# A retention layer and a squared-ReLU feed-forward on one core: another order for the first loads, unread products in TensorE's waits, and two steps moved on ScalarE

## The chip, the core and the metric

The kernel runs on one core of one Trainium2 chip. The metric is the device time of one execution in microseconds (us). Each kernel was executed several times; medians are given with the lowest and the highest. The engines are TensorE (PE in the profile; its weight loads are PEld), VectorE (DVE), ScalarE (ACT), GpSimd (POOL) and SyncE (SP), which issues most loads.

## The reference

```python
# q, k, v: (8, 8, 576, 64) float32;  w_in: (512, 2048) and w_out: (2048, 512) float64
scores = q @ k.T / sqrt(64)                         # for each batch and head
gamma  = 1 - 2.0 ** (-5 - arange(8))                # one per head
ret    = (scores * where(i >= j, gamma ** (i - j), 0)) @ v
x      = ret.transpose(0, 2, 1, 3).reshape(4608, 512)
out    = maximum(x @ w_in, 0) ** 2 @ w_out
```

The decay `gamma ** (i - j)` is split into a factor `gamma ** i` on q and `gamma ** -j` on v. So q has to be multiplied by a table of tokens and heads, and so has v.

## The kernel before

The tokens go through in chunks of 128. For a chunk, TensorE transposes k and q (`turn`), makes the scores (`scores`), and adds up the result from products inside the chunk and a running sum `u` (`retain_a`, `retain_b`, `retain_c`). The first four chunks give the first block of 512 tokens, and only then does the feed-forward have work ("h products", `first_in`). From there on, retention steps and feed-forward steps alternate (`ffn`), with VectorE and ScalarE converting float64 weights between them. A last stage, all of it on the second weight matrix, starts near 602 us.

```python
def load(i):                                   # chunk i, all on SyncE's queue
    for name, src, pool in (("k", k, ld4), ("q", q, ld3), ("v", v, ld4)):
        ...                                    # k and q in three pieces each, v in one
        if i < NCH and name == "q":            # NCH = 5: the q factors, 256 KB a chunk
            nc.sync.dma_start(dq[:, :, c0:c0 + cs], decay_q[:, :, c0:c0 + cs])
    if i == 0:
        nc.sync.dma_start(dv, decay_v)         # the v factors: small

def turn(i):                                   # transposes, then two copies
    ...
    nc.scalar.copy(kT, ...)                                        # ScalarE
    nc.vector.tensor_tensor(qT, ..., dq[...], op=ALU.mult)         # VectorE, scales q

def retain_b(i):
    ...
    # the tiny copy behind which the next products stand ("L458")
    nc.scalar.copy(u_sb[...][:, 0:2, 0:1], xp[0][:, :, cs - CH:cs - CH + 1])

def w_out_parts():                             # conversion of w_out, step by step
    ...
        yield lambda two=two, beside=beside: (two(), beside())     # beside: two ScalarE steps

def ffn(i, half):                              # between the parts of a chunk
    if steps and steps[0][0] == 0:
        step()                                 # four products and ScalarE's relu
        convert(6)                             # conversion of w_in, ScalarE's steps too
        ...

# main loop, first chunks
turn(0)
for i in range(N_CH + 1):
    if i <= N_EARLY:                           # N_EARLY = 4
        ...
        retain_a(i - 1); retain_b(i - 1); retain_c(i - 1)
        scores(i)
        turn(i + 1)
    ...

# last stage: left operands a, four buffers
if n_last in (0, 5, 10):
    fetch_g(n_last // 5)
...
fetch_w2(NP - 1)                               # the last 1.8 MB of weights
fetch_g(3)                                     # the fourth left operand, behind it
```

## Time and profile before

| | before |
|---|---|
| time, first three runs | 1009.67 us (1004.35 to 1010.14) |
| span of the profiled execution | 1004.70 us |
| TensorE busy | 975.3 us, 97% |
| first scores start | 8.29 us |
| first h product starts | 36.41 us |
| ninth h product starts | 42.37 us |
| second stage (later blocks) starts | 114.62 us |
| last product of the second stage ends | 602.25 us |

The last five rows are read from TensorE's timeline, four starts and one end (601.22 + 1.03; the last stage's first product overlaps it, at 602.08). They cut the execution into stages. TensorE is nearly always busy, so a wait of another engine counts only where TensorE stops for it.

These are TensorE's waits in the first 40 us before the change (columns: what waited, what it waited for, us in total, times, longest):

```profile
PE t_ps L373 <- DMA k_ld<-in_k_dram: 4.4, 4, 3.2
PE sc_ps L399 <- DVE qT L381: 2.0, 1, 2.0
PE x_ps L455 <- ACT u_sb L429: 2.0, 4, 0.5
PE x_ps L420 <- ACT u_sb L458: 1.1, 4, 0.3
```

The last two rows are the holes of every chunk, 0.5 and 0.3 us, into which the change puts its unread products.

### The profile page before, as it was taken

The page shows a single profiled execution, that of the slowest core. Times are in us where ns is not written, and L with a number is a line of the kernel's source. Part 1 is how long each engine was busy: PE and PEld are TensorE (multiplying, and loading weights), DVE is VectorE, ACT ScalarE, POOL GpSimd, SP SyncE. Part 2 cuts the span into 40 slices and gives each one's busy share as a digit, 9 for nine tenths or more (in the row PEclk, how much of TensorE's full clock was granted, in tenths as well). Part 3 has the DMA queues.
Part 4 walks back from the last instruction along what each step waited for, and adds up shares of the span by engine and source line. Part 5 has one row for each costly group of instructions (what it writes and reads, how often), then busy time and mean ns, then how long its engine had stood idle before and what let it go on. Part 6 is the DMA issues. An engine that isn't in the chain of part 4 may idle for free.

```text
span 1004.7 us, 24101 instructions
## 1 busy us (share of the span) xinstructions
PE 975.3 (97%) x10376; PEld 862.4 (86%) x10376; DVE 749.7 (75%) x1418; ACT 188.9 (19%) x459; POOL 81.8 (8%) x82
## 2 busy tenths in 40 slices
PE   6999999999999999999999998999999999999998
PEld 4544688888888888788888888999999999999997
DVE  1678797667878888798885776877677677777765
ACT  2344331122222222312311000000000000000000
POOL 1200011011111111111021000000000000000000
PEclk9999999999999999999999999999999999999999
DMA  8974665664786877579566989674764757556351
GB/s 201 241 212 143 183 180 177 171 195 151 207 291 203 239 259 228 139 258 282 150 243 249 401 351 350 252 273 168 252 237 162 273 189 272 187 212 217 119 210 43
DMA packets 187658, 220.34 MB, mean 219 GB/s; under 512 B 119200, under 2 KB 137632, under 8 KB 178592
## 3 DMA queue, kind: packets, MB, share of 16 engines
q1 hardware_dynamic: 187552, 218.81, 66.8%
q8 instruction: 81, 1.33, 0.5%
q14 instruction: 25, 0.20, 0.1%
HBM read 129.39 MB, written 89.39 MB: 218 GB/s over the span
## 4 chain that ended last, share of the span: by engine, by line
PE 87%; DVE 7%; DMA 2%; ACT 2%; SPq 2%; issue 1%; DVEq 0%
PE o_b L800 16%; PE h_b L576 15%; PE o_c L800 11%; PE o_a L800 11%; PE h_a L576 10%; PE h_c L576 9%; PE h_ps L541 6%; PE x_ps L420 3%; PE t_ps L373 2%; PE x_ps L455 2%; DMA a<-g_dram 1%; PE sc_ps L399 1%; DVE room L583 1%; SPq L142 1%; DMA k_ld<-in_k_dram 1%
## 5 line engine op out<-in xcount | busy, mean ns | idle before, releaser
L576 PE MATMUL h_b<-room,w 128*128 128x256 f32 x736 | 177.3, 384 | 1.8 <-DVE room L504 1.2
L576 PEld LDWEIGHTS h_b<-room,w 128*128 128x128 f32 x736 | 137.1, 190 | 22.4 <-DVE room L595 1.4
L800 PE MATMUL o_b<-w,room 128*128 128x128 f32 x1168 | 144.5, 275 | 0.2 <-DVE room L751 0.2
L800 PEld LDWEIGHTS o_b<-w,room 128*128 128x128 f32 x1168 | 137.2, 192 | 0.5 <-DVE room L751 0.4
L800 PE MATMUL o_c<-w,room 128*128 128x128 f32 x1008 | 123.0, 275 | 0.0
L800 PEld LDWEIGHTS o_c<-w,room 128*128 128x128 f32 x1008 | 117.7, 192 | 0.0
L576 PE MATMUL h_c<-room,w 128*128 128x256 f32 x480 | 114.3, 381 | 0.0
L576 PE MATMUL h_a<-room,w 128*128 128x256 f32 x448 | 107.5, 383 | 0.0
L576 PEld LDWEIGHTS h_c<-room,w 128*128 128x128 f32 x480 | 90.5, 190 | 12.5
L576 PEld LDWEIGHTS h_a<-room,w 128*128 128x128 f32 x448 | 83.8, 190 | 11.8
L800 PE MATMUL o_a<-w,a 128*128 128x128 f32 x688 | 85.9, 275 | 2.7 <-DMA a<-g_dram 2.7
L800 PEld LDWEIGHTS o_a<-w,a 128*128 128x128 f32 x688 | 81.3, 192 | 2.9 <-issue 2.9
L593 POOL TENSOR_TENSOR room<-room 128x512 f32<-128x512 f32 x32 | 36.4, 1139 | 435.9 <-ACT room L592 380.7
L583 DVE SCALAR_TENSOR_TENSOR room<-room 128x512 f32<-128x512 f32 x96 | 67.4, 702 | 3.3
L811 ACT COPY r<-o_a 128x128 f32<-128x128 f32 x54 | 14.4, 266 | 276.9 <-PE o_a L800 246.3
L420 PEld LDWEIGHTS x_ps<-ret,v_ld 64*64 64x64 f32 x1152 | 42.5, 143 | 22.8 <-issue 14.1
L420 PE MATMUL x_ps<-ret,v_ld 64*64 64x64 f32 x1152 | 52.4, 234 | 9.1 <-ACT u_sb L458 9.1
L541 PE MATMUL h_ps<-room,w 128*128 128x512 f32 x128 | 59.9, 616 | 0.8 <-ACT room L477 0.7
L595 DVE TENSOR_TENSOR room<-h_b,room 128x512 f32<-128x512 f32 x32 | 22.0, 689 | 42.0 <-PE h_b L576 42.0
L408 POOL TENSOR_TENSOR v_ld<-v_ld,dv 128x512 f32<-128x512 f32 (+1 forms) x40 | 45.0, 1129 | 80.4 <-DMA v_ld<-in_v_dram 67.4
L541 PEld LDWEIGHTS h_ps<-room,w 128*128 128x128 f32 x128 | 24.0, 195 | 27.8 <-issue 25.2
L807 DVE TENSOR_TENSOR small<-o_b,small 128x128 f32<-128x128 f32 x63 | 18.3, 291 | 38.5 <-PE o_b L800 38.4
(94 smaller groups left out, 1369.4 us busy)
## 6 DMA issues: line engine op xcount, KB each, us to landing
g_dram<-room SPq DMA_DIRECT2D x32, 1792.0 KB, 8.1
a<-g_dram SPq DMA_DIRECT2D x43, 1024.0 KB, 7.1
room<-g_dram SPq DMA_DIRECT2D x20, 1024.0 KB, 6.0
w<-w_dram SPq DMA_DIRECT2D x7, 1792.0 KB, 12.1
out_dram<-room SPq DMA_DIRECT2D x18, 512.0 KB, 3.3
v_ld<-in_v_dram SPq DMA_DIRECT2D x32, 256.0 KB, 4.0
w<-in_moe_w_in_dram SPq DMA_DIRECT2D x16, 512.0 KB, 4.9
w<-in_moe_w_out_dram SPq DMA_DIRECT2D x16, 512.0 KB, 4.0
```

Source lines behind the costliest of these rows:

```text
L373: nc.tensor.transpose(p[:, h, j, hp, :], loaded[i][j][rows(h), 2 * hp:2 * hp + 2, :], ident[rows(h), rows(h)])
L408: nc.gpsimd.tensor_tensor(vs[:cs], vs[:cs], dv[:cs, :, ci:ci + 1].to_broadcast([cs, H, D]), op=ALU.mult)
L420: own.append(lambda hp=hp, e=e, b=b: nc.tensor.matmul(x_at(hp, b, h), lhsT=s["vs"][rows(h), 2 * hp + b, :], rhs=s["ret"][rows(h), e, hp, : ...
L455: nc.tensor.matmul(x_at(hp, b, h), lhsT=u[rows(e), hp, :], rhs=s["qT"][rows(e), hp, CH * h:CH * h + CH], start=clears(b, hp // 2), stop=Fa ...
L541: nc.tensor.matmul(p.rearrange("p h t -> p (h t)"), lhsT=w[:, c, :], rhs=xT[0][:, c, :], start=(c == 0), stop=(c == N_DM - 1))
L576: nc.tensor.matmul(p[:, mm, :], lhsT=w[:, c, :], rhs=xs[n][right][:, c, :], start=(j in OPENS and mm == 0 and c == 0), stop=(j in CLOSES a ...
L583: nc.vector.scalar_tensor_tensor(t, t, 0.0, t, op0=ALU.max, op1=ALU.mult)
L593: nc.gpsimd.tensor_tensor(g["A11"], g["A11"], g["A11"], op=ALU.mult)
L595: nc.vector.tensor_tensor(g["A22"], p, p15, op=ALU.add)
L800: nc.tensor.matmul(p, lhsT=s["lefts"][left][:, m, :], rhs=w_out[j][:, m, WO_SLOT[right], :], start=(i in OPENS and m == 0), stop=(i in CLO ...
L807: nc.vector.tensor_tensor(s["u2"], p, s["p1"], op=ALU.add)
L811: nc.scalar.copy(r[:, 0, 0:128], p)
```

## The change

Its intent has five parts. (1) In the first four chunks q is scaled before its transpose by a small table, so that the large table of q factors can be loaded later. Two smaller moves go with it: q is loaded ahead of k, and among the first three chunks one weight piece of 512 KB is fetched instead of two, behind all three. (2) The first k and v are issued by ScalarE's queue beside SyncE's. (3) TensorE makes products that nobody reads ("unread products") in its waits among the first chunks, so that its clock is released from half rate, which the prediction reads from eight equal h products (5.42 us at 36.41 us, 3.70 us at 42.37). (4) Conversion steps of ScalarE are moved so that they don't stand ahead of the tiny copy. (5) The fourth left operand of the last stage is fetched earlier.

```diff
 def load(i):
+    if i == 0:
+        nc.sync.dma_start(dv, decay_v)              # now holds the small q table too
+    if N_EARLY <= i < N_EARLY + NCH:                # the large table, four chunks later
+        nc.sync.dma_start(dq[:, :, c0:c0 + cs], decay_q[:, :, c0:c0 + cs])
-    for name, src, pool in (("k", k, ld4), ("q", q, ld3), ("v", v, ld4)):
+    for name, src in (("q", q), ("k", k), ("v", v)):
     ...
+        issue = nc.scalar if i == 0 and name != "q" else nc.sync
     ...
-        if i < NCH and name == "q":
-            nc.sync.dma_start(dq[:, :, c0:c0 + cs], decay_q[:, :, c0:c0 + cs])

     # start
     for i in range(3):
         load(i)
-        fetch_raw(1 if i else 0)
+    fetch_raw(1)

+def scale_q(i, engine):
+    engine.tensor_tensor(t, t, dv[:, :, NCH + ci:NCH + ci + 1].to_broadcast([C, H, D]), op=ALU.mult)

 # turn
+            elif i < N_EARLY:
+                nc.vector.tensor_copy(to, p[:, :n_h, j, :, :])

 # w_out_parts
-            yield lambda two=two, beside=beside: (two(), beside())
+            yield two, beside                        # held back at the end of a first half
 # ffn
-            step()
-            convert(6)
+            for f in (step, lambda: convert(6)) if half else (lambda: convert(6), step):
+                f()

+def warm(count, wide):                               # unread products
+    t = ps_f.tile([128, 512], F32, tag="f", name="idle_ps")
+    for _ in range(count):
+        if wide:
+            nc.tensor.matmul(t[:, 0:128], lhsT=idle, rhs=idle, start=True, stop=True)
+        else:
+            for b in range(2):
+                nc.tensor.matmul(t[rows(b), 0:64], lhsT=idle[rows(0), rows(b)], rhs=idle[rows(0), 0:64], ...)
 # main loop
+    warm(6, True)
+    scale_q(0, nc.vector)
     turn(0)
     ...
                 retain_a(i - 1)
+                warm(4, False)
                 retain_b(i - 1)
+                warm(4, False)
                 retain_c(i - 1)
     ...
+                if i + 1 < N_EARLY:
+                    scale_q(i + 1, nc.gpsimd)
+                warm(6, False)
                 turn(i + 1)
 # last stage
-            if n_last in (0, 5, 10):
+            if n_last in (0, 5, 10, 15):
                 fetch_g(n_last // 5)
     ...
-    fetch_g(3)
```

Lines of the kernel move by 10 to 38 with the change: the tiny copy L458 is L470 after it, the first copy of qT L381 is L391, the retention products L420 are L432, the h products L541 are L553, the last stage's L800 is L838.

More of the change, by code (lines that the diff above doesn't have):

```diff
@@ L128 @@
     loaded = {}
+    N_EARLY = TOK // C
     def load(i):
         b, ci, c0, cs = chunks[i]
-        got = {}
-        for name, src, pool in (("k", k, ld4), ("q", q, ld3), ("v", v, ld4)):
-            t = got[name] = pool.tile([128, H, D], F32, tag=name, name=f"{name}_ld")
+        got = {name: pool.tile([128, H, D], F32, tag=name, name=f"{name}_ld") for name, pool in (("q", ld3), ("k", ld4), ("v", ld4))}
+        if i == 0:
[3 more added lines that the diff above has]
+        for name, src in (("q", q), ("k", k), ("v", v)):
+            t = got[name]
+            issue = nc.scalar if i == 0 and name != "q" else nc.sync
             at = src[b, :, c0:c0 + cs, :].rearrange("h s d -> s h d")
             if name == "v":
-                nc.sync.dma_start(t[:cs], at)
+                issue.dma_start(t[:cs], at)
             else:
-                nc.sync.dma_start(t[:cs, 0:H // 2, :], at[:, 0:H // 2, :])
+                issue.dma_start(t[:cs, 0:H // 2, :], at[:, 0:H // 2, :])
                 for e in range(2):
-                    nc.sync.dma_start(t[:cs, H // 2 + e::2, :], at[:, H // 2 + 1 - e::2, :])
-            if i < NCH and name == "q":
-                nc.sync.dma_start(dq[:, :, c0:c0 + cs], decay_q[:, :, c0:c0 + cs])
-        if i == 0:
-            nc.sync.dma_start(dv, decay_v)
+                    issue.dma_start(t[:cs, H // 2 + e::2, :], at[:, H // 2 + 1 - e::2, :])
         loaded[i] = [got["q"], got["k"], got["v"]]
@@ L314 @@
     dq = only.tile([128, HP, S], F32, name="dq")
-    dv = only.tile([128, H, NCH], F32, name="dv")
+    dv = only.tile([128, H, 2 * NCH], F32, name="dv")
     exp_bias = const.tile([128, 1], F32, name="exp_bias")
     nc.gpsimd.memset(exp_bias, -896.0 * 2.0 ** 23)
+    idle = only.tile([128, 128], F32, name="idle")
+    nc.vector.memset(idle, 1.0)
     for i in range(3):
         load(i)
-        fetch_raw(1 if i else 0)
+    fetch_raw(1)
     ident = only.tile([128, 128], F32, name="ident")
@@ L333 @@
     u_sb = [only.tile([128, HP, D], F32, name=f"u_sb{j}") for j in range(3)]
-    N_EARLY = TOK // C
     st = {i: {} for i in range(N_CH)}
@@ L363, in clears @@
         return new
+    def scale_q(i, engine):
+        ci, t = chunks[i][1], loaded[i][0]
+        engine.tensor_tensor(t, t, dv[:, :, NCH + ci:NCH + ci + 1].to_broadcast([C, H, D]), op=ALU.mult)
     def turn(i):
@@ L615, in ffn_in @@
         if n >= 3 or n_w2[0] < 3 + 2 * 5:
-            n_w2[0] += 1
-            f = next(w_out_steps, None)
-            f and f()
+            if not (held[0] and type(w_out_next[0]) is tuple):
+                n_w2[0] += 1
+                f = w_out_next[0]
+                w_out_next[0] = next(w_out_steps, None)
+                for f in f if type(f) is tuple else (f,):
+                    f and f()
             if n == N_BLK - 2 and (mp, j) in ((2, 3), (3, 3)):
-                assert f is None
+                assert w_out_next[0] is None
                 fetch_w2(mp - 2)
@@ L626 @@
     w_out_steps = w_out_parts()
+    w_out_next = [next(w_out_steps)]
+    held = [False]
     n_w2 = [0]
@@ L668, in ffn @@
                 break
-        if steps:
+        count = max(1, int(want) - done[0])
+        while steps and count:
+            held[0] = half == 0 and count == 1
             step()
-        while steps and done[0] < int(want):
-            step()
+            count -= 1
+        held[0] = False
+    def warm(count, wide):
[5 more added lines that the diff above has]
+                for b in range(2):
+                    nc.tensor.matmul(t[rows(b), 0:64], lhsT=idle[rows(0), rows(b)], rhs=idle[rows(0), 0:64], start=True, stop=True,
+                                     skip_group_check=True)
+    warm(6, True)
+    scale_q(0, nc.vector)
     turn(0)
@@ L886, in _decays @@
     gv = (gamma[:, None, None] ** -s.astype(np.float64)).transpose(2, 0, 1)
+    order = [h if h < H // 2 else h ^ 1 for h in range(H)]
+    by_s = (gamma[order, None, None] ** s / math.sqrt(D)).transpose(2, 0, 1)
+    gv = np.concatenate([gv, by_s], axis=2)
     return np.ascontiguousarray(gq, dtype=np.float32), np.ascontiguousarray(gv, dtype=np.float32)
```

## The prediction

> **What bounds the kernel now.** I read the page's busy shares first, then its slices, then the table by stretches of time, then what TensorE waited for, and last the timeline around each wait.
>
> ```profile
> span 1004.7 us, 24101 instructions
> ...
> PE 975.3 (97%) x10376; PEld 862.4 (86%) x10376; DVE 749.7 (75%) x1418; ACT 188.9 (19%) x459; POOL 81.8 (8%) x82
> ```
>
> TensorE is busy 975.3 of 1004.7 us, so filling every gap of it is worth 29.4 us at most, and its last product ends some 5 us before the end. A change of the waits is therefore a change of one or two per cent. The table by stretches tells where the gaps are (columns: length, busy time and count for PE, PEld, DVE, ACT, POOL, then granted clock, DMA share, GB/s):
>
> ```profile
> 10.00:15.00 5.00, 3.82 (x85) 3.01 (x88) 0.98 (x2) 1.12 (x3) 1.16 (x2) 1.00 1.02 254
> 20.00:25.00 5.00, 4.27 (x108) 3.67 (x108) 1.49 (x5) 2.33 (x6) 1.34 (x1) 1.00 0.96 234
> 30.00:40.00 10.00, 8.54 (x133) 5.70 (x126) 5.12 (x9) 4.63 (x11) 1.66 (x2) 1.00 0.85 219
> 40.00:50.00 10.00, 10.00 (x53) 4.51 (x51) 7.38 (x13) 3.07 (x5) 2.31 (x2) 1.00 1.02 281
> 200.00:300.00 100.00, 99.98 (x1210) 85.41 (x1210) 74.74 (x125) 22.91 (x51) 14.56 (x14) 1.00 0.66 212
> ```
>
> The first 40 us lose 11.4 us (the stretches of it summed), 40 to 100 lose 3.8, 300 to 500 lose 5.3, around 600 to 620 lose 3, the end 5. Between 120 and 300 nothing is lost. So four places matter. In the first one, the DMA engines are full as well (share 0.92 to 1.02 from 5 to 30 us): the loads are bound there, and TensorE has a second handicap that no share shows:
>
> ```profile
> 7.54 0.69 DVE L381 TENSOR_TENSOR qT<-t_ps,dq 128x512 f32<-128x512 f32 x1 [7.54 <-DMA dq<-in_decay_q_dram]
> ```
> ```profile
> 23.84 0.95 PE L373 MATMUL t_ps<-ident,k_ld 64*128 64x64 f32 x8 [0.27 <-DMA k_ld<-in_k_dram]
> ...
> 36.41 5.42 PE L541 MATMUL h_ps<-room,w 128*128 128x512 f32 x8 [0.68 <-ACT room L477]
> ...
> 42.37 3.70 PE L541 MATMUL h_ps<-room,w 128*128 128x512 f32 x8
> ...
> 46.00 0.46 PE L373 MATMUL t_ps<-ident,k_ld 64*128 64x64 f32 x8
> ```
>
> Eight equal transposes take 0.95 us at 23.84 and 0.46 at 46.00; eight equal products take 5.42 us and then 3.70. Until about 40 us TensorE runs at half its rate, although the granted clock reads 1.00. The first scaled q waits until 7.54 us for the large decay table (dq), which lands after q itself.
>
> The chain puts the start on the issue queue and then on one transfer, the k of the fourth chunk:
>
> ```profile
> 17.64 6.07 DMA k_ld<-in_k_dram
> ```
>
> The other three places, in the waits of TensorE and in the timelines of ScalarE and of the issue queue:
>
> ```profile
> 51.53 0.65 ACT L214 ACTIVATE w<-w 128x512 f32<-128x512 uint32 x1
> 52.07 0.15 ACT L458 COPY u_sb<-x_ps 128x2 f32<-128x2 f32 x1
> ```
> ```profile
> PE x_ps L420 <- ACT u_sb L458: 3.7, 4, 1.1
> ```
> ```profile
> PE o_a L800 <- DMA a<-g_dram: 2.7, 1, 2.7
> ```
>
> The tiny copy L458 releases the next retention products, and it stands in ScalarE's queue behind the weight conversion (L213 0.71 and L214 0.65 us). This costs 3.7 us in 40 to 120, and 3.8 us in 300 to 500 by the same row there. The 2.7 us are the fourth left operand of the last stage: its load is issued at 607.40, behind a 1.8 MB weight load, and lands 14.12 us later by the chain.
>
> [...] the excess 5.42 - 3.70 = 1.72 us is four products at the slow rate (4 x 0.43), or 3.4 us of work. [...] Before, q's first issue is at 2.34 us, after 1.5 us of k's issues, so that is what there is to save.
>
> **The change, part by part.**
>
> *First chunks.* The dq pieces (four of 256 KB and one of 128 KB) leave the front of the queue; the small table goes first, on one queue with q, and k and v of chunk 0 are issued by ScalarE. q is scaled before its transpose, by VectorE for chunk 0 (0.69 us, as L381), by GpSimd for three more (1.06 us each, as L408), off the path if the data is there; L381 becomes a plain copy for four chunks. Chunk 0: q's issue ends near 2.9 us instead of 3.87; it landed 1.9 us after that before, so 4.8; scaling to 5.6; q transposes 1.0 to 6.6; copy 0.7: first scores at about 7.4 instead of 8.29 us. Gain 0.9.
>
> *Unread products.* Before the chunks 12 passes of 128 columns, which lie in the wait of 3.19 us for k. Per chunk 8 + 8 + 12 small products of two passes. They use two column halves side by side, so 28 pairs. A pass of 512 columns takes 3.70 / 8 = 0.46 us fast, so 64 columns take 0.058: 1.6 us a chunk fast, 3.2 us slow (estimates). The real work of a chunk, slow: scores 1.08, transposes 1.78, two inner rounds of 1.1, the outer one 1.14: 6.2 us, which with the waits is the 7.0 us from one chunk to the next (20.17 to 27.18 us). Fast, from 42 to 61 us: 0.69 + 0.76 + 2 x 0.68 + 0.69 = 3.5 us. So a chunk is about 5.2 us if the products release the rate, and about 9.4 if not. I expect release: scores, filler, inner, filler, outer, filler, inner follow each other without a hole for some 7 slow us between transposes[...]. With the first chunk still mostly slow (7.5): scores at 7.4, 14.9, 20.1, 25.3, and the first h product about 5.3 us after the last, at 30.6 instead of 36.41: 5.8 us. The 1.7 us of slow h products go too: 7.5.
>
> Does the DMA let it? Up to the second weight piece 12 loads of 256 KB, two of 512 KB and the table: 4.2 MB, at the 207 GB/s measured over the first 40 us 20 us, plus 2 for the start: 22. The third piece comes 1.0 MB later, at 27, just when VectorE wants it. The dq pieces that were taken out come back before chunks 4 to 8, at 20 to 50 us, where the share is 0.85 to 1.02. So I take off 1.5 us: **6 us** from the front.
>
> *Conversion in 40 to 120.* In the first half-step of each chunk the conversion now goes ahead of the product step, so L213 and L214 run before L458. Comparing ScalarE's order in both programs: before, 10 of 40 copies L458 come directly behind a conversion, four of them in this stage; after, three of 40, none here. Of 3.7 us I take **3**.
>
> *Conversion in 300 to 500.* A step that would end the first half with a conversion is held for the next. Three of the waits (0.33, 1.42, 1.32) lose their cause, one (0.82) stays, and one copy near 462 us newly gets a conversion before it (up to 1 us): **2 us**.
>
> *Last stage.* The fourth left operand is fetched in the last block's 16th of 28 steps, near 580 us, and the DMA has idle time from 596 to 608. So the 2.7 us go: **2.6**.
>
> Sum 6 + 3 + 2 + 2.6 = 13.6 us. The three runs before average 1008.1 us: 994.5.
>
> **Rivals.**
> 1. *TensorE stays slow.* [...] against it is that nothing else stands in the 7 us. Each chunk would then cost 2.4 us more instead of 1.8 less: the front loses 8 or so, and the sum is near zero: 1008 us.
> 2. *The DMA is the bound of the front.* Shares of 0.92 to 1.02 speak for it. Then moved bytes are only paid later: VectorE waits for weight pieces between 30 and 50 us, and the front gives 1 or 2 us: 999 us. Against it: the DMA was half idle for some 3 us near 30 us.
> 3. *The next transfer replaces the last stage's.* The fifth operand's sums already waited 0.79 us at 626.55 for its load, issued at 613.60 into room that a write must leave first. If it is not sooner, only 1.3 us remain: 996 us.
> 4. *All of it without a late weight piece*: 7.5 to 9 in front, 3.7, 3 and 2.7: 989 us.
>
> **Range and chances.** The parts other than the front total 5 to 9 us; the front goes from -8 to +9. The runs before spread over 5.8 us. That makes 987 to 1004 for 8 in 10. Faster by over 2% means under 989.5, which needs the fourth rival: 0.15. Slower by over 2% would need a stall that nothing here points to: 0.02.
>
> **What would show it.** Right: eight transposes of chunk 2 in about 0.5 us instead of 0.95, and the first eight h products in 3.7 us, starting near 31; no wait for dq at the first copy of qT; no wait over 0.4 us of L420 for L458 between 40 and 120; no wait of L800 for the fourth operand. Wrong: first h products still at 5.4 us, or later than 36; VectorE's first conversion step (L205) waiting for its weight load between 25 and 50 us; a new wait near 622 us for the fifth operand.

## The result, and the profile after

| | before | after |
|---|---|---|
| time, four runs each, same rounds | 1008.9 us (1004.35 to 1010.14) | 994.84 us (992.27 to 998.75) |
| span of the profiled execution | 1004.70 us | 990.54 us |

The ratio is 0.9872, with an interval from 0.9825 to 0.9919. A ratio is always the mean time of one kernel's fast runs over that of the other's of the same rounds, so it isn't quite the ratio of the medians. The gain is a little over 1%, and so within the 2% that count as the same.

The changed kernel had nine fast executions, with a mean of 995.2 us and a spread from 992.3 to 998.8. The profiled one is the fastest of the nine, which matters below. One more execution took 1241.73 us at a mean granted clock of 0.754; it was slow from beginning to end, it stayed single, and it isn't used.

The page of the changed kernel, its first lines and its row of instruction loads:

```profile
span 990.5 us, 24582 instructions
...
PE 974.3 (98%) x10612; PEld 866.2 (87%) x10612; DVE 747.5 (75%) x1420; ACT 189.6 (19%) x459; POOL 83.1 (8%) x85
...
q8 instruction: 83, 1.36, 0.6%
```

TensorE has 236 more products (224 records of the small unread ones, two to each, and 12 of the wide ones) and as many more weight loads than before, and yet 1 us less of busy time. What got shorter is the idle time: the span less PE's busy time was 29.4 us and is 16.2 us.

The stages tell where (us; the first two marks are starts, the last two are ends of the last product):

| mark | before | after | stage before | stage after | difference |
|---|---|---|---|---|---|
| ninth h product | 42.37 | 39.07 | 42.37 | 39.07 | -3.3 |
| second stage | 114.62 | 107.25 | 72.25 | 68.18 | -4.1 |
| end of the second stage's products | 602.25 | 591.00 | 487.63 | 483.75 | -3.9 |
| end of the last stage's products | 999.77 | 985.58 | 397.52 | 394.58 | -2.9 |

The table by stretches of time after the change, for the stretches shown of before (length, busy time and count for PE, PEld, DVE, ACT, POOL, then granted clock, DMA share, GB/s), with one stretch more:

```profile
10.00:15.00 5.00, 5.00 (x128) 4.76 (x128) 1.20 (x3) 1.12 (x3) 2.12 (x2) 0.53 1.08 248
20.00:25.00 5.00, 3.48 (x150) 3.21 (x151) 0.95 (x3) 2.75 (x6) 1.06 (x1) 1.00 0.58 146
25.00:30.00 5.00, 5.00 (x154) 4.83 (x148) 4.58 (x8) 2.23 (x6) 1.38 (x1) 0.66 1.01 258
30.00:40.00 10.00, 8.36 (x156) 5.20 (x155) 3.89 (x8) 3.70 (x9) 1.06 (x1) 1.00 0.86 201
40.00:50.00 10.00, 9.92 (x98) 5.07 (x97) 9.79 (x17) 4.78 (x9) 1.06 (x1) 1.00 1.09 321
```

Two things stand out. The unread products fill 10 to 15 us without a hole, but at a clock of 0.53. And 20 to 25 us lose 1.5 us although the DMA engines are only 58% busy there: this hole isn't a transfer. The waits of TensorE in the first 40 us name it:

```profile
PE t_ps L383 <- issue: 1.5, 1, 1.5
PE sc_ps L411 <- DVE qT L391: 1.4, 1, 1.4
PE t_ps L383 <- DMA k_ld<-in_k_dram: 1.2, 1, 1.2
PE x_ps L467 <- issue: 1.1, 2, 0.9
```

"Issue" is a stop in which TensorE waited for nothing that the profile shows. Before the change there was none of any size here. The waits for k, 4.4 us in sum, are down to 1.2, for the most part because unread products now stand in the first of them (without them x2 waits 5.1 us for k); the holes of each chunk are gone; and the stops are new. TensorE's timeline around the first of them (start, length, operation, tiles, count, and in brackets the idle time before it and what ended it):

```profile
20.85 0.87 PE L702 MATMUL idle_ps<-idle 64*64 64x64 f32 x24
21.65 0.40 PE L383 MATMUL t_ps<-ident,k_ld 64*128 64x64 f32 x5
23.57 0.34 PE L383 MATMUL t_ps<-ident,k_ld 64*128 64x64 f32 x3 [1.52 <-issue]
...
34.83 3.70 PE L553 MATMUL h_ps<-room,w 128*128 128x512 f32 x8 [0.68 <-ACT room L489]
...
39.07 3.70 PE L553 MATMUL h_ps<-room,w 128*128 128x512 f32 x8
```

The k of that chunk had landed at 19.18 us, so the eight transposes stop in their middle, with their data there. The first eight h products take 3.70 us instead of 5.42, as predicted, but they start at 34.83 us and not near 31.

The start of VectorE and ScalarE after the change:

```profile
5.88 0.69 DVE L373 TENSOR_TENSOR q_ld<-q_ld,dv 128x512 f32<-128x512 f32 x1 [4.82 <-DMA q_ld<-in_q_dram]
...
7.13 0.58 ACT L389 COPY kT<-t_ps 128x512 f32<-128x512 f32 x1 [2.97 <-PE t_ps L383]
...
7.75 0.69 DVE L391 COPY qT<-t_ps 128x512 f32<-128x512 f32 x1 [1.18 <-ACT kT L389]
```

The wait for the large table is gone, and the first scores still start at 8.50 us instead of 8.29. q is there at 5.76 us, is scaled and transposed, and then the two copies follow one another: VectorE's starts when ScalarE's is about over, which is what its bracket names.

ScalarE near 50 us, where the conversion stood ahead of the tiny copy before:

```profile
47.23 0.60 ACT L557 ACTIVATE room<-h_ps 128x512 f32<-128x512 f32 x1 [1.53 <-PE h_ps L553]
47.73 0.16 ACT L470 COPY u_sb<-x_ps 128x2 f32<-128x2 f32 x1
```

Now the relu stands ahead of the copy, and TensorE has no wait at all between 40 and 120 us in its list. Between 400 and 500 us one is left:

```profile
PE x_ps L432 <- ACT u_sb L470: 1.0, 1, 1.0
```

In the last stage the 2.7 us wait for the fourth operand is gone; in its waits from 590 to 660 us only one of 0.2 us stands.

**Theory and rivals after the result.** The total was as predicted, but the front gave 3.3 us and not 6, in the fastest execution of nine. Theory A: the loads are worth what was predicted or nearly, and the unread products bring nothing or cost, by their own time and the stops. Theory B: the unread products are what gains, and the loads leave the front where transfers bound it before. Theory C for the stops: they have to do with the number of products, because each one is an instruction; against it, that they come from the data or the clock. For the spread: it comes from the front too.

### The profile page after: what moved, and what is told of

It is laid out like the page before. It is cut to its first block, busy times and chain, and to the rows that moved or that the text cites.

```text
span 990.5 us, 24582 instructions
## 1 busy us (share of the span) xinstructions
PE 974.3 (98%) x10612; PEld 866.2 (87%) x10612; DVE 747.5 (75%) x1420; ACT 189.6 (19%) x459; POOL 83.1 (8%) x85
## 4 chain that ended last, share of the span: by engine, by line
PE 94%; DVE 4%; ACT 1%; issue 1%; DMA 0%; SPq 0%; DVEq 0%; ACTq 0%
PE o_b L838 17%; PE h_b L588 17%; PE o_c L838 11%; PE o_a L838 11%; PE h_c L588 11%; PE h_a L588 11%; PE h_ps L553 5%; PE x_ps L432 3%; PE t_ps L383 2%; PE x_ps L467 2%; PE sc_ps L411 2%; PE idle_ps L702 1%; PE u_ps L435 1%; DVE room L595 0%; DMA q_ld<-in_q_dram 0%
## 5 line engine op out<-in xcount | busy, mean ns | idle before, releaser
L838 PE MATMUL o_b<-w,room 128*128 128x128 f32 x1168 | 144.5, 275 | 0.2 <-DVE room L789 0.2
L838 PEld LDWEIGHTS o_b<-w,room 128*128 128x128 f32 x1168 | 137.2, 192 | 0.5 <-DVE room L789 0.4
L838 PE MATMUL o_c<-w,room 128*128 128x128 f32 x1008 | 123.0, 275 | 0.0
L838 PEld LDWEIGHTS o_c<-w,room 128*128 128x128 f32 x1008 | 117.7, 192 | 0.0
L838 PE MATMUL o_a<-w,a 128*128 128x128 f32 x688 | 85.6, 275 | 0.0
L838 PEld LDWEIGHTS o_a<-w,a 128*128 128x128 f32 x688 | 81.2, 192 | 0.1
L553 PE MATMUL h_ps<-room,w 128*128 128x512 f32 x128 | 58.1, 602 | 0.8 <-ACT room L489 0.7
L607 DVE TENSOR_TENSOR room<-h_b,room 128x512 f32<-128x512 f32 x32 | 22.1, 690 | 42.2 <-PE h_b L588 42.2
L432 PEld LDWEIGHTS x_ps<-ret,v_ld 64*64 64x64 f32 x1152 | 40.2, 136 | 13.3 <-issue 11.5
L432 PE MATMUL x_ps<-ret,v_ld 64*64 64x64 f32 x1152 | 49.6, 226 | 1.4 <-ACT u_sb L470 1.4
L420 POOL TENSOR_TENSOR v_ld<-v_ld,dv 128x512 f32<-128x512 f32 (+1 forms) x40 | 43.6, 1092 | 70.7 <-DMA v_ld<-in_v_dram 65.8
L553 PEld LDWEIGHTS h_ps<-room,w 128*128 128x128 f32 x128 | 23.3, 190 | 26.7 <-issue 24.9
```

What stands on the lines that cost most here:

```text
L420: nc.gpsimd.tensor_tensor(vs[:cs], vs[:cs], dv[:cs, :, ci:ci + 1].to_broadcast([cs, H, D]), op=ALU.mult)
L432: own.append(lambda hp=hp, e=e, b=b: nc.tensor.matmul(x_at(hp, b, h), lhsT=s["vs"][rows(h), 2 * hp + b, :], rhs=s["ret"][rows(h), e, hp, : ...
L553: nc.tensor.matmul(p.rearrange("p h t -> p (h t)"), lhsT=w[:, c, :], rhs=xT[0][:, c, :], start=(c == 0), stop=(c == N_DM - 1))
L607: nc.vector.tensor_tensor(g["A22"], p, p15, op=ALU.add)
L838: nc.tensor.matmul(p, lhsT=s["lefts"][left][:, m, :], rhs=w_out[j][:, m, WO_SLOT[right], :], start=(i in OPENS and m == 0), stop=(i in CLO ...
```

## The experiments

Twelve runs were made in three calls, each on another chip; each call shared the runs of the kernel before on its chip. Their medians were 1007.64 us in the first, 1007.68 in the second and 1009.72 in the third. All results were correct. "Without" below means the changed kernel without unread products (x2), the base of y1 to y4 and of z2 to z4. Times of the first two calls are compared as they are, since the kernel before agrees there within 0.04 us; those of the third by their ratios.

| run | time, median (range) | ratio to before |
|---|---|---|
| x1, the changed kernel again | 997.23 with the slow one; fast: 992.48 to 998.04 | 0.9872 [0.9833, 0.9912] |
| x2, no unread products | 991.14 (990.91 to 991.53) | 0.9828 [0.9802, 0.9854] |
| x3, unread products alone on before | 1010.7 (1007.04 to 1011.08) | 1.0023 [0.9992, 1.0054] |
| x4, few wide unread products | 992.04 (991.42 to 993.06) | 0.9837 [0.9811, 0.9864] |
| y1, x2 with the late fetch | 995.68 (994.21 to 996.65) | 0.9867 [0.984, 0.9894] |
| y2, x2 with the old conversion order | 999.11 (998.34 to 999.32) | 0.9904 [0.9884, 0.9925] |
| y3, x2 with the large table early | 994.77 (993.97 to 995.14) | 0.9862 [0.9841, 0.9883] |
| y4, x2 with few products in two places | 992.0 (991.12 to 992.84) | 0.9835 [0.9814, 0.9857] |
| z1, the changed kernel, one more look | 994.0 and 995.47 | 0.985 [0.9818, 0.9882] |
| z2, x2 on one queue | 992.75 (992.19 to 993.01) | 0.9831 [0.9808, 0.9855] |
| z3, x2, nine chunks by the small table | 992.48 (992.38 to 993.78) | 0.9831 [0.981, 0.9851] |
| z4, z3 with y4's products | 992.73 (989.3 to 994.29) | 0.9826 [0.9798, 0.9854] |

### x1: the changed kernel again

No edit.

> The changed kernel once more, as the yardstick of this batch: about 14 us under the kernel before (ratio near 0.987), first h product near 34.8 us (36.4 before), eight h products in 3.7 us, second stage (first product of h_a, h_b or h_c) starting near 107 us (114.6 before). If the gain were only the chip's mood, the ratio would be nearer 1.

The three fast runs were 992.48, 996.42 and 998.04 us. The profiled execution was the slow one of 1241.73 us, so this run gives times only. The spread of 5.6 us is there again; the next run hasn't got it. The kernel before has one as wide (1006.23 to 1012.74 us in this call).

### x2: no unread products

```diff
 def warm(count, wide):
+    return
```

> The changed kernel without any unread product. Theory (they release the rate of TensorE early): the first chunks run slow again, 7 us each, transposes of chunk 2 in 0.95 us, first h product near 36 us, its first eight in 5.4 us; in all some 3 us slower than the changed kernel. Rival (the loads made the whole gain of the front, the products only fill waits that cost nothing): first h product at 34.8 or earlier, since the products' own 1.6 us a chunk go, and the time is the same or a little lower than the changed kernel's.

It is faster: 991.14 us, with all four executions within 0.6 us. That is 4.0 us below the mean of the changed kernel's nine (995.2 - 991.2). So theory A holds for the sign: the unread products cost. The version beats both kernels.

The lengths of the front's pieces show why, from start to start (us):

| piece | before | after | z1 (after, another execution) | x2 without | y1 (x2's front, another execution) | x4 wide |
|---|---|---|---|---|---|---|
| to the first scores | 8.29 | 8.50 | 8.64 | 8.52 | 8.65 | 8.81 |
| first to second scores | 7.00 | 6.76 | 6.61 | 5.63 | 5.64 | 7.68 |
| second to third | 7.21 | 5.12 | 5.20 | 6.01 | 4.86 | 5.08 |
| third to fourth | 7.00 | 7.51 | 8.21 | 4.61 | 4.58 | 6.04 |
| fourth to the first h product | 6.91 | 6.94 | 6.56 | 6.74 | 6.18 | 7.00 |
| first to ninth h product | 5.96 | 4.24 | 5.80 | 6.02 | 5.94 | 4.24 |
| ninth h product at | 42.37 | 39.07 | 41.02 | 37.53 | 35.85 | 38.85 |

Against x2 the unread products win 0.9 us in the third row and 1.8 us in the last of the pieces. They lose 1.1 us in the second row, where they run at the slow rate, and 2.9 us in the fourth, where the stop is. The two losses stand against y1 as well; the 0.9 us do not. The rate rises without unread products too: the record has it full from 21.5 to 28.3 us in x2 and from 16.7 to 30.3 us in y1, then at half until 35.1 and 33.7 us, so that the first h products are slow in both. TensorE's timeline of x2 for the same places:

```profile
9.58 0.69 PE L383 MATMUL t_ps<-ident,k_ld 64*128 64x64 f32 x8
...
20.16 1.08 PE L411 MATMUL sc_ps<-qT,kT 64*64 64x64 f32 x32
21.16 0.58 PE L383 MATMUL t_ps<-ident,k_ld 64*128 64x64 f32 x8
...
23.28 0.69 PE L467 MATMUL x_ps<-qT,u_sb 64*64 64x64 f32 x32 [0.50 <-ACT u_sb L441]
...
31.51 5.48 PE L553 MATMUL h_ps<-room,w 128*128 128x512 f32 x8 [0.68 <-ACT room L489]
...
37.53 3.70 PE L553 MATMUL h_ps<-room,w 128*128 128x512 f32 x8
```

The transposes at 21.16 follow the scores with no idle time: once the loads come in time, there is no hole where 12 of the 28 pairs of passes of each chunk were put. The other 16 stand in holes of 0.50 and 0.28 us. By the prediction's own estimate of 0.058 us for a pair, from the 3.70 us of eight h products, they need 0.93 us at the full rate where 0.78 us are free. The changed kernel has the eight pairs of one hole, 16 records, in 0.63 us at the full rate (17.75 us) and in 1.07 us at half (26.18 us). That the two products of a pair run side by side shows in the 24 records at 20.85 us: 0.87 us, where 24 in a row would take 1.39 us by the same estimate.

The first row has a second lesson. The record of the granted clock shows the rate at full from 21.5 us only, so the transposes at 9.58 us ran at half rate, and they took 0.69 us. The 0.95 us at 23.84 us in the kernel before were thus not the slow clock alone, and a chunk at the slow rate takes 5.6 to 6.0 us (second and third rows) and not 7.0. The rest of the 0.95 is a hole of some 0.2 us between the fourth and the fifth transpose, which fits k arriving in pieces; the profile names no cause for it.

### x3: the unread products alone

On the kernel before: the idle tile, `warm`, and its calls; nothing else.

```diff
+    warm(6, True)
     turn(0)
     ...
                 retain_a(i - 1)
+                warm(4, False)
                 retain_b(i - 1)
+                warm(4, False)
                 retain_c(i - 1)
     ...
+                warm(6, False)
                 turn(i + 1)
```

> The kernel before with only the unread products added. Theory: transposes of chunk 2 in about 0.5 us, the first eight h products in 3.7 us instead of 5.4; k of chunk 3 still lands near 24 us, so the first h product comes at 34 to 36; 2 to 4 us under the kernel before. Rival (without the earlier loads TensorE idles on transfers and falls slow again): eight h products in 5.4 us and no gain, or up to 3 us of loss from the products' own time.

1010.7 us, a ratio of 1.0023: no gain; the interval holds 1, so a loss isn't shown either. The first eight h products take 3.70 us, but the first starts at 38.54 us instead of 36.41, and the second stage at 115.14 instead of 114.62. TensorE's waits in its first 40 us:

```profile
PE u_ps L425 <- issue: 2.2, 1, 2.2
PE sc_ps L401 <- DVE qT L383: 1.7, 1, 1.7
...
PE sc_ps L401 <- issue: 0.8, 1, 0.8
...
PE t_ps L375 <- issue: 0.4, 1, 0.4
```

The waits for k, which were 4.4 us, have left the list, and 3.4 us of stops have come into it.

### x4: few wide unread products

One matmul of 64 times `count` columns replaces the `2 * count` small ones, for the same number of column passes and a fraction of the instructions. That puts theory C to the test.

```diff
-                for b in range(2):
-                    nc.tensor.matmul(t[rows(b), 0:64], lhsT=idle[rows(0), rows(b)], rhs=idle[rows(0), 0:64], ...)
+                pass
+        if not wide:
+            nc.tensor.matmul(t[:, 0:64 * count], lhsT=idle, rhs=idle_w[:, 0:64 * count], ...)
```

> The changed kernel with each group of 8 or 12 small unread products replaced by one of 256 or 384 columns over the whole array, of about the same time, in 4 instructions instead of 32 or 48. In the changed kernel TensorE stands 1.52 us at 22.05 and 0.93 at 31.57 us although what it needs has landed, each time just after a 16 KB instruction load. Theory[...]: both stops vanish or shrink under 0.3 us, the window of slow rate from 25 to 28.4 goes, and the first h product starts 3 to 4 us earlier, near 31. Rival (the stops are waits for a transfer or another engine that the profile does not name): they stay at 1.5 and 0.9, first h product near 34.8.

992.04 us, 3.2 us below the changed kernel's mean and 0.9 above x2. The stops get smaller and don't go:

```profile
23.52 0.48 PE L705 MATMUL idle_ps<-idle_w,idle 128*128 128x384 f32 x1 [0.79 <-issue]
...
28.23 0.57 PE L413 MATMUL sc_ps<-qT,kT 64*64 64x64 f32 x23 [0.29 <-issue]
```

The rate stays full from 15.4 us on, and the spread is 1.6 us. The first h product starts at 34.61 us and not near 31, where the expectation put it if the stops were what cost. That the stops shrink speaks for theory C, but the number of products alone doesn't set them: y4 below has 16 product records more than x2 and a stop of 1.28 us, z4 one of 1.14. In x2 and y1, which have no unread products, no stop is over 0.2 us, although the rate was full from 21.5 and 16.7 us; so the full rate alone doesn't bring them. The trace has something that fits. A load of 16 KB on the instruction queue starts 1.06 us before the stop of 1.52 us and 1.65 us before that of 0.93 us (20.99 and 29.92 us in the profiled execution); in z1 it is 0.9 and 1.5 us, but in x3 0.5 us before the stop of 2.15 us and in x4 1.8 and 2.7 us. The loads go with TensorE's instructions by their number: 2 x 10612 products and weight loads to 83 loads are 255.7 for each; before, 2 x 10376 to 81 are 256.2. But the distance varies, other loads in the front bring no stop (those at 16.39 and 25.15 us), and no record says that TensorE waited for instructions. That the stops are such waits fits, and isn't shown.

### y1: the fourth operand late again

```diff
-            if n_last in (0, 5, 10, 15):
+            if n_last in (0, 5, 10):
     ...
     fetch_w2(NP - 1)
+    fetch_g(3)
```

> The changed kernel without unread products (991.1 us, its four executions within 0.6 us, so a better base than the changed kernel's 992 to 999), with the fourth left operand of the last stage fetched late again as before. Theory: TensorE waits again about 2.7 us for it and the last stage takes 397.5 us instead of 394.6: 994. Rival (the fifth operand limits in either case): under 1.3 us of difference.

995.68 us, 4.5 us over x2. The last stage is 399.12 us long instead of 394.57. The wait is back, as a row of the waits from 590 us on:

```profile
PE o_a L839 <- DMA a<-g_dram: 2.7, 1, 2.7
```

That is 2.7 of the 4.5 us. The rest is in the table by stretches:

```profile
600.00:650.00 50.00, 47.32 (x409) 47.16 (x409) 33.85 (x79) 3.98 (x15) 0.00 (x0) 0.97 0.79 292
```

The mean granted clock is 0.97 there. Its record has one window at half rate, 610.6 to 614.0 us, right where the wait ended, at 610.25 us: half of 3.4 us, or 1.7 us lost. In the profiled execution of the kernel before, the same wait was not followed by half rate: the record is at full from 39.9 to 1002.5 us. Whether half rate followed it in all four executions of y1 is not shown; the profiled one is the slowest of them.

Up to the last stage y1 is the same program as x2:

```profile
29.91 5.40 PE L553 MATMUL h_ps<-room,w 128*128 128x512 f32 x8 [0.68 <-ACT room L489]
...
35.85 3.70 PE L553 MATMUL h_ps<-room,w 128*128 128x512 f32 x8
```

Both start 1.6 to 1.7 us earlier than in x2, and yet the second stage starts at 107.10 us, 0.6 us later than x2's 106.52. TensorE waits 1.5 us for VectorE's qT near 45 us, and a window at half rate follows (47.4 to 50.8 us). So single profiles of the front differ by this much with no edit at all.

### y2: the old order of the conversions

```diff
-            yield two, beside
+            yield lambda two=two, beside=beside: (two(), beside())
     ...
-            for f in (step, lambda: convert(6)) if half else (lambda: convert(6), step):
+            for f in (step, lambda: convert(6)):
                 f()
     ...
-            held[0] = half == 0 and count == 1
```

> The same base with both moves of ScalarE's conversion undone. Theory: the waits of L420 for L458 (by the numbers of the kernel before) return, about 3.3 us between 40 and 107 us and 3.9 between 107 and 591: 998 to 999. Rival (only the waits seen in the trace of before count, 3.7 and 3.1, and the rest of what the stages gained is luck of the run): 996 to 998.

999.11 us, 8.0 us over x2, the largest of all parts. The first stage, from the ninth h product, is 72.56 us long instead of 68.99, and the second 487.66 instead of 483.75: 3.6 and 3.9 us. The waits of TensorE, from 40 to 120 us:

```profile
PE x_ps L432 <- ACT u_sb L470: 2.5, 3, 1.0
PE sc_ps L411 <- DVE qT L393: 1.2, 1, 1.2
```

and from 300 to 550 us:

```profile
PE x_ps L432 <- ACT u_sb L470: 4.3, 5, 1.4
PE h_b L588 <- DVE room L607: 0.5, 1, 0.5
```

In x2 the first stretch has only 0.7 us for qT L393 and 0.2 us for a weight, and the second has 1.4 us for the copy and 0.6 for L607. ScalarE's timeline has the cause, the conversion ahead of the copy as before the change:

```profile
46.98 0.67 ACT L218 ACTIVATE w<-w 128x512 f32<-128x512 uint32 x1
47.53 0.14 ACT L470 COPY u_sb<-x_ps 128x2 f32<-128x2 f32 x1
```

### y3: the large table early again

The q of the first chunks is still scaled by the small table; the large one is loaded right behind q again, for nothing but its bytes. It isn't quite the old order: k came ahead of q and of the table then, and here, from the second chunk on, each piece of the table is ahead of its own chunk's k.

```diff
-        if N_EARLY <= i < N_EARLY + NCH:
-            nc.sync.dma_start(dq[:, :, c0:c0 + cs], decay_q[:, :, c0:c0 + cs])
     ...
+            if i < NCH and name == "q":
+                nc.sync.dma_start(dq[:, :, c0:c0 + cs], decay_q[:, :, c0:c0 + cs])
```

> The same base, q still scaled from the small table, but the pieces of the large table issued again right behind the first five chunks' q. Theory (the front is bound by transferred bytes): first scores still near 8.5 us, but k of chunk 3 lands at about 23.5 instead of 19.2 us and the first h product comes at 35 to 36 us instead of 31.5: 994 to 995. Rival (the gain came from not waiting for the table, not from its bytes): first h product within 1 us of 31.5, time within 1 us of 991.

994.77 us, 3.6 us over x2. The first h product starts at 35.12 us instead of 31.51, again 3.6 us. TensorE's waits in the first 50 us, of y3:

```profile
PE t_ps L382 <- DMA k_ld<-in_k_dram: 7.5, 5, 3.4
```

and of x2:

```profile
PE t_ps L383 <- DMA k_ld<-in_k_dram: 5.1, 3, 3.6
```

The waits for k grow by 2.4 us. So 3.6 of the 4.9 us by which x2's first h product comes before that of the kernel before are those of transfers: the bytes of the large table are no longer ahead of k. What made the other 1.3 us, the weight piece that was moved or the small table, no run tells apart; x2 and y1 differ by 1.6 us with no edit. The bytes now come with the loads of chunks 4 to 8; z3 below tries whether they cost anything there.

### y4: few unread products, in the two holes alone

On x2, with x4's wide form: 192 columns after `retain_a`, 128 after `retain_b` (0.59 us at 20.89 us and 0.49 at 22.20 in the profiled execution), none at the start and none before `turn`.

```diff
                 retain_a(i - 1)
+                warm(3, False)
                 retain_b(i - 1)
+                warm(2, False)
                 retain_c(i - 1)
```

> The same base with wide unread products in the two waits of each early chunk alone (192 and 128 columns[...]), none before the first chunk and none after the scores, which are no wait. Theory (the rate is worth something[...]): the first eight h products in 3.7 us, first h product at or before 31.5, so 1 to 3 us under the base: 988 to 990. Rival (the front is bound by transfers and by VectorE's conversion once the loads are moved): first h product no earlier, time 990 to 992.

992.0 us, a ratio of 0.9835 against 0.9828: no gain over x2. The first eight h products take 3.70 us, the rate is released for them, and the ninth h product starts at 36.08 us against 37.53 in x2; but y1, with x2's front, has it at 35.85. The second stage starts at 107.68 us, 1.2 us later than in x2 and 0.6 later than in y1. Its waits in the first 50 us:

```profile
PE t_ps L385 <- DMA k_ld<-in_k_dram: 5.8, 4, 3.6
PE sc_ps L413 <- DVE qT L395: 1.8, 1, 1.8
...
PE sc_ps L413 <- issue: 1.3, 1, 1.3
```

A faster TensorE gets to the next wait sooner: VectorE's qT near 45 us comes late, as in y1, and as there a window at half rate follows (47.1 to 50.5 us). A stop of 1.3 us comes in even with these few products.

### z1: one more look at the changed kernel

No edit.

> The changed kernel again for a second profile: its executions spread over 6 us (992.3 to 998.8) where the one without unread products stays within 0.6. Theory (its spread is the front: where the rate of TensorE rises and falls[...] differs from run to run): in an execution of 995 or more, the ninth h product starts later than 39.1 us by about the surplus over 992.3, and the stretches from 107 us on have the same lengths (483.8 and 394.6). Rival: the surplus lies in the later stages at a lower granted clock.

994.0 us in the profiled execution (the expectation asked for one of 995 or more), which lets two executions of the same program be compared. The ninth h product starts at 41.02 us against 39.07, and the second stage at 109.01 us against 107.25; both later stages are as long as they were (483.74 and 394.57 us). Its stop:

```profile
PE t_ps L383 <- issue: 1.8, 1, 1.8
```

It is 0.3 us longer here, and the clock record has a half-rate window from 35.0 to 38.4 us, on the first h products, that the other execution hasn't. So the difference of these two, 1.7 us, is all in the front. That the slower executions, up to 998.8 us, differ there as well is inferred: none of them has a profile.

### z2: one queue

```diff
-            issue = nc.scalar if i == 0 and name != "q" else nc.sync
+            issue = nc.sync
```

> The changed kernel without unread products, with k and v of chunk 0 issued by the same queue as all else, behind q. Theory ([...] the first scores wait for both k and q): k of chunk 0 lands about 1.5 us later, first scores at 9.5 to 10 instead of 8.5 us, but later chunks are bound by the bytes, so the first h product moves by less than 1 us and the time by less than 1 us: 991 to 992. Rival (the chain from chunk to chunk carries the delay): 992.5 or more.

A ratio of 0.9831 against x2's 0.9828: the same. The first scores start at 8.42 us against 8.52; 9.5 to 10 was expected. So what the second queue saves doesn't show in the first scores.

### z3: nine chunks by the small table

Since x2's VectorE waits for weight pieces, the large table is moved out of the way altogether:

```diff
+    N_SMALL = N_EARLY + NCH
-        if N_EARLY <= i < N_EARLY + NCH:
+        if N_SMALL <= i < N_SMALL + NCH:
     ...
-            elif i < N_EARLY:
+            elif i < N_SMALL:
                 nc.vector.tensor_copy(to, p[:, :n_h, j, :, :])
     ...
+            if i + 1 < N_SMALL:
+                scale_q(i + 1, nc.gpsimd)
```

> The changed kernel without unread products, with q of the first nine chunks scaled on GpSimd from the small table, so that the large table's pieces come with chunks 9 to 13, after 60 us, when the DMA share is 0.5 to 0.8. Theory (once the loads are moved the front is bound by the landing of the weight pieces: VectorE's L209 waits 1.74 us at 29.5 and 1.50 us at 43.2 for them): the 0.9 MB fewer bring the pieces some 3 to 4 us earlier, these waits go, and the second stage starts 1 to 2.5 us earlier: 988.5 to 990. Rival (TensorE at its slow rate is the bound): no change within 1 us of 991.

A ratio of 0.9831: no gain. VectorE's waits in the first 50 us, of x2:

```profile
DVE w L209 <- DMA w<-in_moe_w_in_dram: 3.2, 2, 1.7
```

and of z3:

```profile
DVE w L210 <- DMA w<-in_moe_w_in_dram: 1.2, 2, 0.9
```

The wait for weights shrinks by 2 us as meant, but the first eight h products take 6.22 us instead of 5.48 (the record has half rate from 26.9 to 37.1 us), and the second stage starts at 107.29 us, 0.8 us later than in x2 and 0.2 later than in y1. So the arrival of the weights alone is not what bounds the front now.

### z4: both together

z3's edit with y4's products.

> The same with the wide unread products in the two waits of each early chunk. Theory: with the weight pieces early, the rate is worth something at last: first eight h products in 3.7 instead of 5.4 us and the second stage 2 to 4 us earlier than without nine and unread products (106.5): 987 to 989. Rival: the unread products never pay, same as the run before or slower.

A ratio of 0.9826, from 989.3 to 994.29 us; it can't be told from x2. The first eight h products take 5.40 us, and not 3.7 as expected: the rate was at half from 25.4 to 35.6 us. The profiled front: ninth h product at 38.10 us, second stage at 106.75. What limits the stage that ends between 106.5 and 107.7 us in all these versions is not settled; the versions that make one part of it faster get a wait in another, of the size of the gain.

## Why the prediction was right, and where its steps failed

The total was right, 994.5 predicted and 994.84 measured, inside the range. Three of its four parts were the right mechanism. That the sum held was luck: the front gave 2.7 us less than predicted, and the other parts 3.3 us more.

| part | predicted | stage in the fastest profile | by undoing the part on x2 |
|---|---|---|---|
| front, loads and unread products | 6 | 3.3 | 3.6 for the loads, -4.0 for the products |
| conversions, 40 to 120 us | 3 | 4.1 | 3.6 |
| conversions, 300 to 500 us | 2 | 3.9 | 3.9 |
| last stage | 2.6 | 2.9 | 4.5 |
| sum | 13.6 | 14.2 | 11.6 |

The last column compares medians with x2 (for the conversions, stage lengths of y2 with those of x2), and for the products the mean of the changed kernel's nine executions with the mean of x2's. Its positive terms, with the two conversion terms taken as the 8.0 us of y2's median, sum to 16.1 us. x2's median lies 16.5 us under that of the kernel before of its call, so the parts add up within half a microsecond. The 4.5 us of the last stage hold the rate drop of y1, though, which the profile of the kernel before hasn't got; from profile to profile x2's stages gain 4.8, 3.3, 3.9 and 2.9 us, together the 14.9 us between the two spans.

**Unread products: this step failed, and with it the sign.** "I expect release" was right as to the rate: it rose (full from 4.5 to 7.9 us and from 14.7 us), and for one chunk it did just what was worked out (5.12 us from the second scores to the third, 5.2 predicted). But it was not needed there: y1 takes 4.86 us without the products. What raises the rate is not shown: without them it rose as well, at 21.5 us in x2 and at 16.7 in y1. What is left to them is the first h products, 3.70 us instead of 5.4 to 5.5, and in z1 not even that (5.26). What failed is "follow each other without a hole". TensorE stopped for 1.52 us after the third scores and for 0.93 us after the fourth with nothing awaited, and behind the first stop the rate fell to half again for one window (25.0 to 28.4 us), in which 16 of their records took 1.07 us instead of 0.63. And the holes were smaller than the products put into them, once k came in time. None of the four rivals was this one; the nearest, the first, has TensorE stay slow.

**The 7.0 us of a chunk: misread.** "Nothing else stands in the 7 us" was wrong. At half rate and with the loads moved, a chunk took 5.6 to 6.0 us in x2. The 0.95 us of eight transposes held some 0.26 us beyond half rate, which alone is 0.69 us; waiting for pieces of k fits, and isn't shown.

**First scores: the 0.9 us didn't come.** q landed at 5.76 us and not at 4.8, so the scaling ended a microsecond later than worked out, and after the transposes stood not one copy of 0.7 us but two in a row. z2 shows that the second queue wasn't worth anything either (8.42 us on one queue, 8.52 on two).

**The bytes: right, and undersized by the second rival's fear only a little.** y3 puts them at 3.6 us. The second rival was right in part: in x2 VectorE does wait for weight pieces, 1.7 and 1.5 us, near 29 and 43 us. In the changed kernel TensorE comes later, and that sign didn't show.

**Conversions: right, terms undersized.** Where 3 and 2 us stood, 3.6 and 3.9 were measured. In the second stretch the copy's waits fell from 3.9 us in 300 to 500 us to 1.0, which is 2.9; the prediction had left 0.8 us and up to 1 more standing, and one of 1.0 us stands, at 491 us. Over the whole second stage they fell from 4.3 to 1.4 us, and a wait for VectorE's room from 1.2 to 0.9 (L504 before, L516 after). The rest of the 3.9 us doesn't show as a wait; which instruction gave it is open.

**Last stage: right, and the third rival did not come.** (The 3 us that the prediction read around 600 to 620 lie up to 700 us; by 620 it is 1.3.) The wait for the fourth operand went and none for the fifth took its place. The part is worth 2.9 us from profile to profile. On x2 it is worth 4.5, because in y1 the wait was followed by a window at half rate (610.6 to 614.0 us), which the prediction did not have.

## What to carry to other kernels

Fill a wait with unread products only when the wait stays there after the other parts of the change, and price each product at the slow rate as long as the rate isn't known to be up (24 records of the small ones took 1.50 us at half rate, at 9.40 us, and 0.87 at full, at 20.85). When an operation is longer than its twin elsewhere, look at when its data landed before blaming the clock. And undo the parts of a change one by one even when the total is as predicted: here the best version was the change without one of its parts. Before a microsecond is read from a profile, compare two executions of the same program: here the first h product moved by 1.6 us between x2 and y1 although nothing in their fronts differs.

## What the records of the clock and of the instruction loads showed

- Half rate came after short stops: after one of 1.52 us, in a stretch with 16 transposes (window from 25.0 to 28.4 us), and after a wait of 2.68 us in y1 (610.6 to 614.0 us). In the kernel before it did not come after a wait of 2.7 us at the same place. The recorded stretches of one rate are 3.41 us at full, 6.83 at half, 10.24 at full, 3.41 at half and 962.56 at full in the changed kernel, and 962.56 at full in the kernel before. All are 3.41 us or a multiple of it; only the last of each execution (1.63 and 4.25 us, at half) isn't.
- Eight transposes took 0.69 us in a half-rate window (the changed kernel, 10.83 us) and 0.46 us in a full one (16.57 us), so their time changes with the rate.
- Stops of 0.8 to 1.8 us with nothing awaited came 0.9 to 1.7 us after 16 KB instruction loads in two executions of the changed kernel, and 0.5 to 2.7 us after them in other kernels with unread products. Whether the loads cause them is open.
- A profile's granted clock reads 1.00 until the first recorded switch. Before the change, the first record is at 39.9 us, and the column read 1.00 while eight h products took 5.42 us instead of 3.70.
